# Attention forward and backward with the rows of three heads ordered 32, 32, 32, 8, 8, 8: V and dO rows of heads 0 to 23 copied from the projection pass instead of transposed on PE

## The chip, the cores and the metric

The kernel runs on one core of a Trainium2 chip. The metric is the device time of one execution in microseconds (us), as the median of several executions. Stage times and waits come from the trace of one profiled execution of each kernel.

The engines are called PE (matrix products and transposes), PEld (its weight loads), VectorE (DVE in the profile), ScalarE (ACT), GpSimd (POOL) and SyncE (SP, which only issues transfers). Each works through its own list in order, and they wait for each other by semaphores.

## The reference

A block with segment-wise attention that carries a memory of 8 rows from segment to segment, then a gated linear unit; the kernel computes the output and the gradients of eleven inputs.

```python
S, D, H, E = 2048, 512, 32, 128;  M, T = 8, 32;  L = M + T = 40   # 64 segments
for s in range(64):                                  # attention A
    h = concat([mem, x[s*T:(s+1)*T]])                # 40 rows
    q, k, v = (einsum('btd,dhe->bhte', h, W) for W in (Wq, Wk, Wv))
    p = softmax(where(mask, q @ k.T * E**-0.5, -1e9))
    o = einsum('bhte,hed->btd', p @ v, Wo)
    mem = o[:M]                                      # the next segment needs it
    out.append(o[M:])
x = x + ga * A(layernorm(x) * (1 + ca) + sa)         # ca, sa, ga, ... from silu(c) @ w_mod
x = x + gb * B(layernorm(x) * (1 + cb) + sb)         # B: (sigmoid(h@w_gate) * (h@w_up)) @ w_down
outputs = (x, *vjp(grad_out))
```

Segments depend on each other through `mem` in the forward pass and through its gradient in the backward pass, so both passes are 64 steps one behind the other. What one step's chain takes, the kernel takes 64 times.

## The kernel before

Three heads with 40 rows each make one group of 120 rows; 32 heads (and one pad) make 11 groups. In the forward pass V is projected with rows on partitions (`RA["v"]`), turned by PE into columns per head (`VT`, which the backward pass needs too), and eight of the eleven groups are turned back by PE, this time in group order, into `Vst`, the stationary side of P.V:

```python
                if norms:
                    norms.pop()()                 # GpSimd: Pst of segment s-1 times 1/denominator
                proj("v", 0, "act")
                proj("v", 1, "dve")
                ...
                if 1 <= s4 <= 3:
                    p1(s // nseg_t + P1_AHEAD, s4)   # layer norm of the next tile; s4 = s % 4
                proj("k", 0, "act")
                ...
                self.pop_later()
                st_exp(0)
                vst(0)                            # 4 PE transposes, copied out by VectorE
                st_exp(1)
                vst(1)                            # 4 more
                vst(2)                            # the last three groups
                den(0)
                pv(0)
```

Two pieces of work that come up again are the normalisation on GpSimd and step 2 of the layer norm on VectorE:

```python
                def norm(s=s, Pst=Pst, rden=rden):
                    nc.gpsimd.tensor_tensor(Pst[0:120, :, :], Pst[0:120, :, :], rden..., op=ALU.mult)
                    nc.sync.dma_start(self.PS[s], Pst[:])
            def scale():
                nc.vector.tensor_scalar(xh[:], st["x0"][:], mean, rstd, op0=ALU.subtract, op1=ALU.mult)
                nc.vector.tensor_tensor(xh[:], xh[:], ca1_bc[:], op=ALU.mult)
```

The backward pass does the same with dO (`RAd`, `dOT`, `dOst`). ScalarE copies the turned columns to `dOT`, VectorE multiplies them with O, PE sums these products with a matrix of minus ones on top of dP, and VectorE makes dS:

```python
                to_heads("act", tp[:], 4, 4, 0, 32, 0)   # two ScalarE copies a half: heads 0-23, last heads
                prod(0)          # VectorE: OT *= dOT, groups 0-3
                dp(0)            # PE: dO.V
                dost(0)          # PE: 4 transposes of dO, copied out by ScalarE
                prod(1)
                prod(2)
                ds(0)            # PE: -sum(dO*O); VectorE: dS
```

The softmax here doesn't subtract the row's maximum and nothing guards it: scores larger than these inputs give would overflow.

Of the kernel before, what the change touches and what calls it, by code (L numbers as in the profile page):

```python
# [40 lines left out]
class K:  # L41
# [209 lines left out]
    def pin(self, i0):  # L251

        last = {}
        for ins in self.traced()[i0:]:
            e = ins.engine
            if e in last:
                self.tc.add_manual_dep(ins, last[e].name, mybir.DependencyInfo(
                    mybir.DependencyClass.NoSync, mybir.DependencyReason.DATA), reason="program order")
            last[e] = ins

# [133 lines left out]
    def phase2(self):  # L394
# [13 lines left out]
        with ExitStack() as ctx:  # L408
# [4 lines left out]
            nc.vector.tensor_copy(maskT[0:120, :], self.maskT[:, :])  # L413
# [29 lines left out]
            RB = {x: ptiles("RB" + x, 1, w=9 * 128)[0] for x in "vkq"}  # L443
# [18 lines left out]
            with tc.tile_pool(name="p0", bufs=1) as p0:  # L462
                p1(0, 0)
# [55 lines left out]
            def to_heads(eng, xt, src, i0, n, r0, w, o):  # L519

                s4 = src.rearrange("p i (j r) -> p i j r", r=32)
                d = xt[:, 120 * i0:120 * (i0 + n)].rearrange("p (i j r) -> p i j r", j=3, r=L)
                self.evac(eng, d[:, :, :, r0:r0 + w], s4[:, :, 0:3, o:o + w])
                for a0, n0, dst in ((0, 3, 0), (3, 3, L), (6, 2, 2 * L)):
                    lo, hi = max(a0, i0), min(a0 + n0, i0 + n)
                    if lo < hi:
                        d = xt[:, 960:1320].rearrange("p (i r) -> p i r", r=120)[:, lo - a0:hi - a0]
                        self.evac(eng, d[:, :, dst + r0:dst + r0 + w], s4[:, lo - i0:hi - i0, 3, o:o + w])

            def rows_out(rows, dram, s0, ns):  # L530

                if ns == 1:
                    nc.sync.dma_start(dram[s0, 0:120, 0:8, :].rearrange("(j r) g e -> j r (g e)", r=L)[:, 0:32],
                                      rows[0:96, 0:1024])
                    nc.sync.dma_start(dram[s0, 0:120, 8:11, :].rearrange("(hl r) g e -> r hl (g e)", r=L)[0:32],
                                      rows[96:128, :].rearrange("r (hl x) -> r hl x", hl=3))
                    return
                for j in range(3):
                    nc.sync.dma_start(dram[s0:s0 + 4, L * j + 32:L * j + L, 0:8, :].rearrange("s q g e -> s q (g e)"),
                                      rows[32 * j:32 * j + 32, 0:1024])  # L540
                for hl in range(3):
                    nc.sync.dma_start(dram[s0:s0 + 4, L * hl + 32:L * hl + L, 8:11, :].rearrange("s q g e -> s q (g e)"),
# [5 lines left out]
            def b_pieces(t):  # L548

                bt = btails[t] = {}  # L550

                def proj_b(x, hf):
                    hb = hxs[t][1]
                    pass_half(x, hf, lambda c: hb[:, c, :, :].rearrange("p s q -> p (s q)"), RB[x], ("act", "dve")[hf])
                    if hf == 1 and x != "v":
                        rows_out(RB[x], DR[x], t * nseg_t, nseg_t)

                def turn_b(x):
                    bt[x] = btp.tile([128, 8, 128], BF16, name="b_cols" + x)
                    tps = [turn_half(RB[x], hf) for hf in range(2)]  # L560
# [37 lines left out]

            tails_in("vk", 0)
            i0 = len(self.traced())  # L600
            for s in range(NS):
# [10 lines left out]
                def proj(x, hf, eng):  # L612
                    pass_half(x, hf, lambda c: hT[:, c, :], RA[x], eng)
                    if hf == 1 and x != "v":
# [57 lines left out]
                def outproj(h0, h1):  # L672
                    if at_ps[0] is None:
                        at_ps[0] = psp.tile([128, 512], F32, name="at_ps", tag="p")
                    for h in range(h0, h1):
                        off = (h // 3) * GW + (h % 3) * L
                        self.col_mm(at_ps[0], OT[:, off:off + 32], Wo[:, h, :], n_at[0], H)
                        n_at[0] += 1

                if norms:  # L680
                    norms.pop()()
                proj("v", 0, "act")
                proj("v", 1, "dve")
                if s == NS - 1:
                    nc.sync.dma_start(self.w_up, io["B_w_up"].rearrange("(c p) f -> p c f", p=128))
                    self.mod_bc(None, 2, "", t=self.bcs[2])
                    self.mod_bc(None, 3, "", t=self.bcs[3])
# [4 lines left out]
                if s == NS - 1:  # L692
                    nc.sync.dma_start(self.w_down, io["B_w_down"].rearrange("(fc p) d -> p fc d", p=128))
                    self.mod_bc(None, 4, "", t=self.bcs[4])
# [13 lines left out]
                if s == NS - 1:  # L708
                    self.mod_bc(None, 5, "", t=self.bcs[5])
                    nc.sync.dma_start(self.w_gate, io["B_w_gate"].rearrange("(c p) f -> p c f", p=128))  # L710
                self.pop_later()
                st_exp(0)
                vst(0)
                st_exp(1)
                vst(1)
# [5 lines left out]
                nc.sync.dma_start(Pst[:], ET[:, :], transpose=True)  # L721
                if mod_r:
# [19 lines left out]
                if s + 1 < NS:  # L742
                    tails_in("kvq", s + 1)
# [12 lines left out]
                if s == NS - 1:  # L756
                    self.glu_first = self.glu_load(0, nc.scalar)
# [9 lines left out]
            self.pin(i0)  # L767

    def glu_tiles(self):
# [3 lines left out]
        self.w_gate = self.flat(Wv, 0, n).rearrange("p (c f) -> p c f", c=DC)  # L773
        self.w_up = self.flat(Wv, n, n).rearrange("p (c f) -> p c f", c=DC)
        self.w_down = self.flat(Wk, 0, n).rearrange("p (c d) -> p c d", c=FC)
        self.bcs = {2: self.flat(Wv, 2 * n, 2 * D, F32), 3: self.flat(Wv, 2 * n + 2 * D, 2 * D, F32),
                    4: self.flat(Wk, n, 2 * D, F32), 5: self.flat(Wq, 2 * n, 2 * D, F32)}
        self.w_gateT = self.flat(Wq, 0, n).rearrange("p (c d) -> p c d", c=FC)
        self.w_upT = self.flat(Wq, n, n).rearrange("p (c d) -> p c d", c=FC)
        self.ring_x0 = [self.flat(Wq, 2 * n + 2 * D + i * D, D) for i in range(2)]  # L780
        self.ring_a = [self.flat(Wk, n + 2 * D + i * D, D) for i in range(6)]
        self.ring_dout = [self.flat(Wk, n + 8 * D + i * D, D) for i in range(7)]
# [10 lines left out]
    def phase3(self):  # L793
# [9 lines left out]
        with ExitStack() as ctx:  # L803
            wtp = ctx.enter_context(tc.tile_pool(name="p3wt", bufs=1, reuse_waits="tile"))
            psM = ctx.enter_context(tc.tile_pool(name="p3psM", bufs=4, space=PSUM, reuse_waits="tile"))
# [1050 lines left out]
```

## Time and profile before

| | us |
|---|---|
| time beside the prediction, median of 3 | 3344.8 |
| all 4 runs of it beside the changed kernel, median | 3350.5 (3339.9 to 3357.9) |
| profiled execution | 3355.7 |
| forward pass, first to last output projection | 1042.0 |
| last row fold to first gate product | 39.3 |
| GLU, first gate product to last accumulation | 362.9 |
| GLU weight gradients, to first dO pass | 199.2 |
| backward pass, first to last dO pass | 1031.8 |
| last dO pass to last gradient product of Wo | 196.4 |
| the rest of the weight gradients | 420.1 |

Each stage is the time between the starts of two named PE instructions in the trace. The prediction shows the busy times and PE's waits. First, two GpSimd groups of the page (busy us and mean ns of one, then its idle time ahead of them and who ended it), then all multiplies of `xh` by `ca_bc` on VectorE (count, shortest, median and longest in ns, first and last start).

```profile
L65 POOL COPY vT<-b_colsv 128x24 bf16<-128x24 bf16 (+2 forms) x256 | 49.7, 238 | 581.3 <-DMA VT<-vT 572.2
L760 POOL TENSOR_TENSOR Pst<-Pst,rden 120x1408 bf16<-120x1408 bf16 x64 | 162.2, 2534 | 57.1 <-DMA Pst<-ET 26.7
```

```profile
L365 DVE TENSOR_TENSOR xh<-xh,ca_bc x16: 691/693/694, 14.3 to 938.4; 128x512 f32<-128x512 f32 x16
```

GpSimd spends 572 us waiting for the store of `VT` to land, so all that stands behind it, the normalisation of 2.53 us included, comes late in a segment. The VectorE multiply takes 0.69 us each of its 16 times. Last, VectorE in one backward segment, whose first dO product started at 2195.26 (start, length, what, idle before):

```profile
2197.69 0.42 DVE L63 CAST RAd<-pass_ps 128x256 bf16<-128x256 f32 x1 [0.65 <-ACT RAd L61]
2198.03 0.22 DVE L295 COPY dh_rb<-dh_tp 128x128 bf16<-128x128 bf16 x1
2198.17 0.40 DVE L1335 TENSOR_TENSOR OT_l<-dOT,OT_l 128x480 bf16<-128x480 bf16 x1
2199.48 0.67 DVE L1335 TENSOR_TENSOR OT_l<-dOT,OT_l 128x480 bf16<-128x480 bf16 x2 [0.92 <-ACT dOT L61]
2200.22 0.69 DVE L1360 SCALAR_TENSOR_TENSOR dS<-dp_ps,Pst_l 128x512 bf16<-128x512 f32 x1
```

The first product starts 2.91 us into the segment, ahead of the wait for ScalarE's second half, and the first dS at 4.96.

### The profile page before, as it was taken

Reading aid. Unit: us, or ns where it says so; the run is one execution under the profiler, and the core shown is the slowest. Engines: PE = TensorE matmul, PEld = TensorE weight load, DVE = VectorE, ACT = ScalarE, POOL = GpSimd, SP = SyncE. Lnnn points to the kernel's source line nnn. Section 1 sums busy time; section 2 is a strip of 40 time slices with the busy share of each in tenths; the row PEclk is TensorE's granted clock in tenths of the full one; section 3 lists DMA queues with packets and bytes.
Section 4 is the critical chain, followed back from the end, with each engine's and each line's share of the span. In section 5 each row is a group of like instructions: output and inputs, shape, how many; then the busy total and the mean of one; then the engine's idle time right before and its main releaser. Section 6 shows DMA issues by size and latency. Waiting matters only on the chain. (4 is left out here: it accounts for less than half of the span.)

```text
span 3355.7 us, 97380 instructions
## 1 busy us (share of the span) xinstructions
PE 3060.2 (91%) x39662; PEld 1791.3 (53%) x39662; DVE 1644.5 (49%) x4158; ACT 1225.7 (37%) x2842; POOL 1061.3 (32%) x2262
## 2 busy tenths in 40 slices
PE   6999999999998699988989999999999988999999
PEld 3566666565555344444555555555555543445454
DVE  5666666666665567653244445555554442322221
ACT  3444554444444333322134444444444430100111
POOL 2344443333333355540122222222222221332321
PEclk8999999999999899999999999999999998999999
DMA  8788877878777788887779999999999999877685
GB/s 280 156 164 162 161 163 162 158 159 158 155 154 153 201 201 199 203 242 246 228 186 240 245 242 242 246 241 249 243 243 242 239 240 230 242 198 208 181 228 161
DMA packets 862317, 692.22 MB, mean 206 GB/s; under 512 B 562198, under 2 KB 737574, under 8 KB 861740
## 3 DMA queue, kind: packets, MB, share of 16 engines
q1 hardware_dynamic: 768624, 503.21, 67.5%
q0 software_dynamic: 39488, 135.58, 12.0%
q10 hardware_dynamic: 53756, 47.19, 5.3%
q8 instruction: 312, 5.11, 0.7%
q14 instruction: 137, 1.12, 0.1%
HBM read 292.29 MB, written 275.02 MB: 169 GB/s over the span
## 5 line engine op out<-in xcount | busy, mean ns | idle before, releaser
L1663 PE MATMUL gps<-rows,hrows 128*128 128x512 bf16 (+2 forms) x2160 | 417.0, 355 | 0.0
L1663 PEld LDWEIGHTS <-hrows 128*128 128x128 bf16 x2160 | 211.2, 98 | 204.2
L222 PEld LDWEIGHTS <-hT 128*32 128x32 bf16 x6144 | 179.5, 97 | 173.4 <-issue 39.6
L65 POOL COPY vT<-b_colsv 128x24 bf16<-128x24 bf16 (+2 forms) x256 | 49.7, 238 | 581.3 <-DMA VT<-vT 572.2
L63 DVE CAST ot<-gps 128x512 bf16<-128x512 f32 (+3 forms) x76 | 48.2, 635 | 340.8 <-PE gps L1663 231.4
L272 DVE TENSOR_TENSOR dh_lo<-dh_ps,dh_hi 128x256 bf16<-128x256 f32 x128 | 48.4, 420 | 316.3 <-ACT dh_hi L268 316.3
L760 POOL TENSOR_TENSOR Pst<-Pst,rden 120x1408 bf16<-120x1408 bf16 x64 | 162.2, 2534 | 57.1 <-DMA Pst<-ET 26.7
L61 ACT ACTIVATE ot<-gps 128x512 bf16<-128x512 f32 (+3 forms) x75 | 41.2, 550 | 360.0 <-PE gps L1663 260.8
L1667 POOL DMA_DIRECT2D out_dram<-ot x108 | 81.2, 752 | 286.1 <-DVE ot L63 143.2
L222 PE MATMUL pass_ps<-Wv,hT 128*32 128x512 bf16 x2048 | 126.0, 388 | 29.7 <-ACT hT L752 29.7
L1381 POOL DMA_DIRECT2D DVR<-rows_x x64 | 34.5, 540 | 371.9 <-DMA rows_x<-dVT 371.9
L222 PE MATMUL pass_ps<-WoT,dyT 128*32 128x512 bf16 x2048 | 124.1, 384 | 27.9 <-ACT dyT L1466 27.9
L61 ACT ACTIVATE dQT<-g_ps 128x512 bf16<-128x512 f32 (+1 forms) x192 | 94.0, 562 | 151.5 <-issue 149.2
L1673 PE MATMUL gps5o<-WoT,rows 128*128 128x512 bf16 x600 | 134.2, 385 | 4.4 <-DMA rows<-OSR 4.4
L662 DVE TENSOR_TENSOR Ost<-or_ps,rden 120x512 bf16<-120x512 f32 (+1 forms) x192 | 124.3, 647 | 21.7 <-PE dc_ps L639 1.7
L1360 DVE SCALAR_TENSOR_TENSOR dS<-dp_ps,Pst_l 128x512 bf16<-128x512 f32 (+1 forms) x192 | 118.3, 644 | 24.0 <-PE dp_ps L1358 19.5
L222 PE MATMUL pass_ps<-Wk,hT 128*32 128x512 bf16 x2048 | 123.8, 382 | 0.0
L222 PE MATMUL pass_ps<-Wq,hT 128*32 128x512 bf16 x2048 | 122.4, 379 | 0.0
L211 PE MATMUL at_ps<-Wo,OT 128*32 128x512 bf16 x2048 | 122.3, 380 | 0.0
L211 PE MATMUL dh_ps<-WkT,dKT 128*32 128x512 bf16 x2048 | 122.3, 380 | 0.0
L211 PE MATMUL dh_ps<-WvT,dVT 128*32 128x512 bf16 x2048 | 122.3, 380 | 0.0
L211 PE MATMUL dh_ps<-WqT,dQT 128*32 128x512 bf16 x2048 | 121.6, 379 | 0.0
(383 smaller groups left out, 7115.9 us busy)
## 6 DMA issues: line engine op xcount, KB each, us to landing
OSR<-Ost SPq DMA_DIRECT2D x64, 352.0 KB
OT<-OT SPq DMA_DIRECT2D x64, 352.0 KB
PS<-Pst SPq DMA_DIRECT2D x64, 352.0 KB
OT_l<-OT SPq DMA_DIRECT2D x64, 352.0 KB
Pst_l<-PS SPq DMA_DIRECT2D x64, 352.0 KB
DVR<-rows_x POOLq DMA_DIRECT2D x64, 352.0 KB, 4.5
DKR<-rows_x POOLq DMA_DIRECT2D x64, 352.0 KB, 4.9
DQR<-rows_x POOLq DMA_DIRECT2D x64, 352.0 KB, 3.7
```

The costliest lines, as they stand in the source:

```text
L61: return nc.scalar.activation(out, in_, AF.Copy)
L63: return nc.vector.tensor_copy(out, in_)
L65: return nc.gpsimd.tensor_copy(out, in_)
L211: self.nc.tensor.matmul(ps[32 * j:32 * j + 32, :], lhsT=lhsT, rhs=w, start=(n < 4), stop=(n >= total - 4), tile_position=(0, 32 * j))
L222: self.nc.tensor.matmul(ps[32 * j:32 * j + 32, :], lhsT=lhs(c), rhs=rhs, start=(c == 0), stop=(c == DC - 1), tile_position=(0, 32 * j))
L272: nc.vector.tensor_tensor(lo[:], ps[:, 256 * h:256 * h + 256], parts[h][:], op=ALU.subtract)
L662: nc.vector.tensor_tensor(part3(Ost, pi)[0:120, 0:n, :], or_ps[0:120, 0:n, :], rden[:, pi * PG:pi * PG + n].unsqueeze(2).to_broadcast([120 ...
L760: nc.gpsimd.tensor_tensor(Pst[0:120, :, :], Pst[0:120, :, :], rden[:, :].unsqueeze(2).to_broadcast([120, G, 128]), op=ALU.mult)
L1360: nc.vector.scalar_tensor_tensor(out=part3(dS, pi), in0=ps[:, 0:n, :], scalar=cfg.scale, in1=part3(Pst, pi), op0=ALU.mult, op1=ALU.mult)
L1663: nc.tensor.matmul(ps[:, 0:ng * E], lhsT=hrows[:, tp_, c * 128:(c + 1) * 128], rhs=rows[:, tp_, 0:ng * E], start=(tp_ == 0), stop=(tp_ == ...
L1667: nc.gpsimd.dma_start(outw[c * 128:(c + 1) * 128, h0:h0 + 3 * (ng - 1) + 1:3, :], ot[:, 0:ng * E].rearrange("p (h e) -> p h e", e=E))
L1673: nc.tensor.matmul(ps[:], lhsT=rows[:, tp_, gg * E:(gg + 1) * E], rhs=dyrows[:, tp_, :], start=(tp_ == 0), stop=(tp_ == NTP - 1))
```

## The change

Its intent: with the 120 rows of a group ordered as 32 memory-and-token rows of three heads and then their 8 last rows, the first 96 rows are in `Vst` exactly as the projection pass puts them on partitions. GpSimd copies them over, the 24 tail rows come by three small transfers, and 8 PE transposes with their copies go, in the forward pass and again for dO in the backward pass. The row stores of Q and K become contiguous. At the seams between stages several loads and waits move. The core of it:

```diff
-                if norms:
-                    norms.pop()()
                 proj("v", 0, "act")
+                nc.gpsimd.tensor_copy(Vst[0:96, 0:512], RA["v"][0:96, 0:512])
                 proj("v", 1, "dve")
+                nc.gpsimd.tensor_copy(Vst[0:96, 512:1024], RA["v"][0:96, 512:1024])
+                if norms:
+                    norms.pop()()
 ...
                 st_exp(0)
-                vst(0)
                 st_exp(1)
-                vst(1)
                 vst(2)
 ...
+                    v_tails(s + 1)          # three transfers of 8 rows x 1024
 ...  rows_out: 3 x 32 x 1024 becomes 96 x 1024
-  nc.sync.dma_start(dram[s0, 0:120, 0:8, :].rearrange("(j r) g e -> j r (g e)", r=L)[:, 0:32], rows[0:96, 0:1024])
+  nc.sync.dma_start(dram[s0, 0:96, 0:8, :].rearrange("r g e -> r (g e)"), rows[0:96, 0:1024])
 ...  backward pass
-                d = dOT[:, 960 + L * i0:960 + L * (i0 + n)]...
-                self.evac(eng, d[:, :, r0:r0 + w], s4[:, :, 3, o:o + w])
+                for g in range(3):                       # last heads: two pieces a half
+                    lo, hi = max(3 * g, i0), min(3 * g + 3, i0 + n, 8)
+                    if lo < hi:
+                        self.evac("pool" if eng == "pool" else "dve", ...)
 ...
+                    nc.gpsimd.tensor_copy(dOst[0:96, 512 * hf:512 * hf + 512], RAd[0:96, 512 * hf:512 * hf + 512])
 ...
                 dp(0)
-                dost(0)
                 prod(1)
 ...
                 dp(1)
-                dost(1)
```

Cut here: the last segment issues its loads on other queues (GLU weights on GpSimd's, rows on SyncE's); the GLU's memory plan and a fifth PSUM buffer; the staging of the attention weights; the first product of the Wo gradients split in three parts, with its rows loaded in pieces; and a pin of the order of SyncE's and ScalarE's loads in the weight gradients.

## The prediction

> **What bounds the kernel now.** I read the page first, then busy time by stage, then PE's waits stage by stage, then PE beside ScalarE and VectorE inside one segment. From the page:
>
> ```profile
> PE 3060.2 (91%) x39662; PEld 1791.3 (53%) x39662; DVE 1644.5 (49%) x4158; ACT 1225.7 (37%) x2842; POOL 1061.3 (32%) x2262
> PEclk8999999999999899999999999999999998999999
> ```
>
> PE is the bound on average, and nothing else is near; but its clock dips three times, at the seams between stages. Busy time by stage (window and its length, PE, PEld, DVE, ACT, POOL in us, then clock, DMA share, GB/s):
>
> ```profile
> 60.00:1105.00 1045.00, 957.47 (x16895) 625.65 (x16896) 633.40 (x1997) 512.06 (x1282) 403.46 (x1076) 1.00 0.78 160
> 1105.00:1700.00 595.00, 518.93 (x3023) 263.70 (x3026) 307.30 (x546) 166.01 (x288) 231.76 (x266) 0.95 0.77 212
> 1700.00:2776.00 1076.00, 985.10 (x16512) 607.43 (x16504) 531.96 (x1251) 468.54 (x1151) 266.00 (x671) 0.99 1.02 241
> 2776.00:3355.00 579.00, 567.21 (x2833) 278.24 (x2833) 142.72 (x279) 62.90 (x90) 150.41 (x204) 0.99 0.77 208
> ```
>
> These are attention forward (64 segments, 16.3 us each), the GLU, attention backward (64 segments, 16.8 us each) and the weight gradients. PE idles 88, 76, 91 and 12 us in them. The waits of PE, taken window by window (total us, times, longest):
>
> ```profile
> PE tps L648 <- DVE Ost L662: 37.7, 109, 0.6
> PE pass_ps L222 <- ACT hT L752: 28.6, 60, 0.8
> ...
> PE ao_b_ft L281 <- ACT ao_b_hi L268: 14.8, 1, 14.8
> ...
> PE acc_ps L1006 <- POOL pr_ga L1000: 9.6, 12, 1.5
> PE mm L909 <- DVE du L934: 5.3, 11, 1.1
> ...
> PE gps L1031 <- DMA Wk<-HHROWS: 7.2, 1, 7.2
> PE pass_ps L222 <- POOL dyb L1244: 4.7, 1, 4.7
> ...
> PE dh_tps L211 <- POOL dh_tail L1732: 10.6, 1, 10.6
> PE gps5o L1673 <- DMA WoT<-zrow: 4.7, 1, 4.7
> ```
>
> Inside a segment the waits are short and recur (a dependent chain through VectorE or ScalarE); at the seams there are four single waits of 5 to 15 us. Now one forward segment, first PE, then ScalarE, then VectorE (start, length, what):
>
> ```profile
> 612.25 0.43 PE L648 MATMUL tps<-ident,vT 128*128 128x128 bf16 x4
> ...
> 613.01 0.55 PE L648 MATMUL tps<-ident,vT 128*128 128x128 bf16 x7
> 613.40 0.24 PE L639 MATMUL dc_ps<-ones,ET 128*128 128x1 bf16 x4
> ...
> 612.50 0.60 ACT L629 ACTIVATE ET<-st_ps 128x480 bf16<-128x480 f32 x1
> ...
> 613.43 0.42 DVE L63 COPY Vst<-tps 128x512 bf16<-128x512 bf16 x1 [0.24 <-PE tps L648]
> ```
>
> The reader sees that 7 transposes take 0.39 us from their start to the next block's, so 0.056 us each; that the exponential of the first score tile ends at 613.10, only 0.30 us before the denominators start; and that VectorE is still copying a V tile when they do.
>
> **What the Trainium skill says.** "TensorE: Matmul & The Clock Gate", Back-to-back issue gap and Part 1: a 128-column matmul costs N/2.4 + 2.5 ns when warm, and about 3.4 us of idling halves the clock. The trace agrees: 56 ns per transpose, and the dips of the clock follow the waits of 14.8 and 10.6 us. "GPSIMD Engine Reference", 4.1 Engine selection: one-input work is roughly at line rate there. The trace agrees: a Pool copy of 264 columns takes 0.41 us and one of 96 columns 0.27 us, so I estimate 0.65 us for 512. "SBUF — State Buffer", Who interferes with whom: a VectorE instruction with two SBUF inputs contends with a Pool instruction that reads SBUF; no line of this profile shows it yet. "DMA: Bandwidth & Descriptors", on why a DMA increments its semaphore by 16: a DMA runs on the largest k up to 16 that divides the slowest dimension of both sides. The row stores of K and Q go from 3x32x1024 to 96x1024, so from 3 engines to 16; the profile doesn't name engines, so it can't confirm this.
>
> **The change part by part.** The compiled programs differ by 1,023 matmuls: 64 segments x 8 transposes x 2 directions, less one added for the mask. The ceiling is 1,024 x 0.056 = 57 us.
>
> *Forward segments.* Removed: 8 transposes (0.45 us PE) and two VectorE copies (0.83 us). Added: two Pool copies of 96x512 (1.3 us) and three small Pool DMAs (0.54 us each, as its other DMA issues take): 2.9 us of Pool, busy 6.3 of 16.3 us now. Pool has room, and PV comes over 5 us after the V pass, so I put nothing of it on the path. But PE doesn't get all of 0.45: the denominators can't start before the exponential is out, at about 613.2, so 0.2 us earlier. VectorE, free of its copies, starts the reciprocal and the first product about 0.3 us earlier, and the three products of 0.69, 0.69 and 0.56 us with their reciprocals set the end. I take 0.32 us x 63 = 20 us, and 4 more for segments where VectorE also serves the next tile's layer norm: 24 us.
>
> *Forward to GLU.* ScalarE sits behind DMA issues that wait for buffers, so PE waits 14.8 us. Those loads go to the sync queue a segment earlier, the weights to Pool's queue. From the end of the forward part (1105.3) to the first GLU matmul (1140.8) are 35.5 us. I estimate 15 to 16: about 10 of transposes that stay, 5 for layer norm and its DMA transpose. The three weights, 5.5 MB at the stage's 214 GB/s, take 26 us and then set the start unless issued 10 us before the seam. Gain 20 us.
>
> *GLU.* The order of the program puts the accumulation that waited for Pool's pr_ga behind the next gate products, and there is a fifth PSUM buffer. A steady iteration takes 20.5 us, of which PE works 18.9. I take 1 us x 13 = 13 us.
>
> *GLU weight gradients, start of backward.* The 7.2 us wait for HHROWS and the 4.7 us wait for dyb go, with some 3 us at half clock behind them, less 1 for loads that now show: 14 us.
>
> *Backward segments.* Removed: 8 transposes (0.45 us) and two ScalarE copies (1.1 us). Added: Pool as before, and four small VectorE copies for the last heads (some 0.16 us each). VectorE lies on the path: products, then dS of 0.69, 0.65 and 0.5 us, then the last transposes of dS. Following one segment by hand I get the three dS done 0.1 us earlier to 0.1 later and the gradient matmuls 0.25 us earlier; a quarter of the segments, where ScalarE also evacuates the tails, should gain 0.5. 64 x 0.31 = 20 us.
>
> *Backward to weight gradients.* Waits of 10.6 (tail copies behind a DMA issue on Pool), 4.7 (zero rows) and 4.4 us (rows<-OSR), each followed by half clock: 40 matmuls there take 402 ns each where 216 is usual. Of the 25 us I expect 19; loading the next rows takes the rest.
>
> Set-up adds about 1 us. Sum: 24 + 20 + 13 + 14 + 20 + 19 - 1 = 109 us. 3344.8 - 109.8 gives **3235 us**, 3.3% less.
>
> **The rivals.** (1) Pool becomes the bound. Its forward order is tails of K, V, Q, then V copies, then the norm; the V tails wait 542 us in total (9 us per segment) for the store of VT. If that landing comes no earlier, Q's tails and then the V copies arrive just at the scores, which already waited on Pool three times (1.5 us in all). For: slack there is some 0.6 us. Against: the stores spread over more engines. It would give back 0.3 to 0.6 us per segment: 3255 to 3270. (2) The chains through VectorE and ScalarE hide all of the transposes: both segment gains vanish, only the seams count, 3280. Against: VectorE is itself relieved in the forward part. (3) DMA: share 1.02 in the backward part. Against: PE waited for no DMA there. If it limits, 20 us go: 3255. (4) The seams don't shrink, as weights or rows land late: 3265 to 3275. Upward, full transposes and full seams would make 3195.
>
> **Range and chances.** No single rival brings it over 3278, the 2% line; two together do. 8 in 10: 3195 to 3285. Faster by over 2%: 0.86; within 2%: 0.13; slower: 0.01.
>
> **What would show it.** Right: forward and backward stages shorter by about 24 and 20 us; PE's wait on VectorE's Ost unchanged or larger; no PE wait over 5 us at the first, second and last seam; GLU iterations near 19.4 us. Wrong: PE waits on Pool for Vst, dOst or qT; on a DMA in the backward part; a forward stage as long as before; a first gate product later than 20 us after the last forward product.

## The result, and the profile after

| | before | after |
|---|---|---|
| median, 4 runs each | 3350.5 | 3385.6 |
| range | 3339.9 to 3357.9 | 3380.7 to 3390.6 |
| ratio | | 1.0107, 95% interval 1.0072 to 1.0143 |

Ratios, here and below, are the mean time of one kernel's runs over the mean of the other's runs of the same rounds, so not quite the ratio of the medians. The change made the kernel 1.1% slower where 3.3% faster was predicted. By stage, from the two profiled executions:

| stage | before | after | predicted | measured |
|---|---|---|---|---|
| forward pass | 1042.0 | 1049.8 | -24 | +7.7 |
| to first gate product | 39.3 | 40.0 | -20 | +0.6 |
| GLU | 362.9 | 355.4 | -13 | -7.5 |
| GLU weight gradients | 199.2 | 197.0 | -14 | -2.2 |
| backward pass | 1031.8 | 1046.4 | -20 | +14.6 |
| to the end of the Wo gradients | 196.4 | 211.8 | -19 | +15.5 |

Forward code that is the same in three kernels below took 1048.2 to 1050.0 us, so differences of 2 us in that stage are scatter; for the kernel before, two such profiles gave 1042.0 and 1048.7. So the loss in the forward pass is somewhere between nothing and 8 us. Backward code that is the same took 1042.3 to 1046.5 us against a single 1031.8 before, so that loss, 10 to 15 us, is clear. The GLU scatters more: its code before the change took 362.9 and 356.5 us in two profiles, the changed code 342 to 358 in all the kernels below, and the GLU weight gradients took 193 to 204 in all kernels. The -7.5 and -2.2 lie within that.

The page of the changed kernel and its stages (windows cut at the ends of the stages, columns as in the prediction):

```profile
PE 3033.4 (90%) x38639; PEld 1729.5 (51%) x38639; DVE 1670.1 (49%) x4292; ACT 1136.6 (34%) x2586; POOL 1442.3 (43%) x3038
```

```profile
60.00:1109.00 1049.00, 942.58 (x16367) 590.79 (x16355) 628.50 (x1869) 508.79 (x1282) 586.25 (x1391) 0.99 0.58 162
1109.00:1702.00 593.00, 517.82 (x3099) 265.92 (x3099) 310.45 (x552) 167.82 (x291) 231.78 (x270) 0.95 0.79 212
1702.00:2773.00 1071.00, 971.78 (x15972) 578.45 (x15965) 559.71 (x1507) 382.31 (x893) 456.37 (x1116) 1.00 1.05 243
2773.00:3384.00 611.00, 570.01 (x2833) 278.54 (x2832) 143.29 (x279) 61.98 (x90) 154.12 (x209) 0.97 0.82 202
```

PE is busy 27 us less (the prediction put the transposes that went at 57), and yet the span is longer: PE waits more. In the forward pass the DMA share fell from 0.78 to 0.58 at the same GB/s. PE's waits over the whole kernel:

```profile
PE tps L680 <- DVE Ost L694: 35.6, 97, 0.7
PE turn_ps L231 <- DVE RA0q L63: 31.7, 14, 2.3
PE dp_ps L1406 <- DVE OT_l L1383: 27.4, 65, 0.9
...
PE mm L945 <- DVE du L966: 18.6, 13, 2.8
PE tp L862 <- DVE Wq L63: 17.8, 3, 16.9
...
PE acc_ps L1610 <- DMA dhb<-DHB: 15.3, 3, 9.0
PE gps5o L1737 <- DMA rows<-OSR: 14.1, 1, 14.1
...
PE wtp L1208 <- DMA won<-in_A_Wo_dram: 6.8, 2, 4.4
...
PE wtp L1195 <- DMA wn<-in_A_Wk_dram: 6.0, 3, 3.4
...
PE wtp L1195 <- DMA wn<-in_A_Wv_dram: 3.8, 2, 3.3
```

The old seam waits (14.8, 10.6, 7.2, 4.7 us) are gone or, in the case of the 7.2, down to 2.7. In their place stand waits that were not there: 14 times 2.3 us for VectorE's copy of Q, a wait in nearly every backward segment for the products dO*O (0.4 us on average, 0.9 at most), and single waits for weights, rows and transfers at each seam.

**The forward pass.** By segment number modulo 4, over the later segments, a segment took 16.79, 16.28, 16.38, 16.49 us before and 16.21, 15.95, 17.85, 15.70 after. Three classes gain 0.33 to 0.79 us (0.32 predicted); one, the class s mod 4 = 2, loses 1.5 us. In such a segment, first GpSimd, then VectorE:

```profile
485.16 0.61 POOL L713 COPY Vst<-RA0v 96x512 bf16<-96x512 bf16 x1 [1.99 <-ACT RA0v L61]
486.13 0.86 POOL L715 COPY Vst<-RA0v 96x512 bf16<-96x512 bf16 x1 [0.36 <-DVE RA0v L63]
486.96 2.53 POOL L790 TENSOR_TENSOR Pst<-Pst,rden 120x1408 bf16<-120x1408 bf16 x1
```

```profile
485.98 0.54 DVE L374 TENSOR_SCALAR xh<-x,mv,rstd 128x512 f32<-128x512 bf16 x1
486.56 3.49 DVE L375 TENSOR_TENSOR xh<-xh,ca_bc 128x512 f32<-128x512 f32 x1
489.97 0.68 DVE L63 CAST RA0k<-pass_ps 128x512 bf16<-128x512 f32 x1
490.57 0.67 DVE L63 CAST RA0q<-pass_ps 128x512 bf16<-128x512 f32 x1
```

The multiply that took 0.69 us before takes 3.49 us: it ends 0.56 us after GpSimd's normalisation, which itself takes its usual 2.53, although it had started 0.41 us before the normalisation, while GpSimd's second V copy still ran (0.86 us, against 0.61 for the first). So it is in 14 of the 16 tiles. Both read two SBUF tensors. VectorE then copies K and Q out 2.8 us late, and PE waits for them. The same view as before, over all 16 tiles:

```profile
L375 DVE TENSOR_TENSOR xh<-xh,ca_bc x16: 692/3490/3492, 14.7 to 951.8; 128x512 f32<-128x512 f32 x16
```

**The backward pass.** VectorE in a segment that started at 2202.83:

```profile
2205.75 0.29 DVE L63 COPY dOT<-turn_ps 128x96 bf16<-128x96 bf16 x2
2205.96 0.21 DVE L305 COPY dh_rb<-dh_tp 128x128 bf16<-128x128 bf16 x1
2207.12 0.29 DVE L63 COPY dOT<-turn_ps 128x64 bf16<-128x64 bf16 x2 [0.94 <-ACT dOT L61]
2207.32 0.97 DVE L1383 TENSOR_TENSOR OT_l<-dOT,OT_l 128x480 bf16<-128x480 bf16 x3
2208.21 1.95 DVE L1408 SCALAR_TENSOR_TENSOR dS<-dp_ps,Pst_l 128x512 bf16<-128x512 f32 x3
```

The four small copies of the last heads stand ahead of the products. The second pair waits for ScalarE's copy of the second half, so even the first product, which needs only the first half, starts 4.49 us into the segment instead of 2.91, and dS at 5.38 instead of 4.96.

**The seam to the GLU.** GpSimd of the changed kernel:

```profile
1129.13 2.53 POOL L790 TENSOR_TENSOR Pst<-Pst,rden 120x1408 bf16<-120x1408 bf16 x1 [22.61 <-DMA Pst<-ET]
...
1133.34 2.28 POOL L897 TENSOR_TENSOR db<-Wv 128x512 bf16<-128x512 bf16 x2
...
1140.18 1.16 POOL L897 TENSOR_TENSOR db<-Wk,Wv 128x512 bf16<-128x512 bf16 x1 [3.51 <-DMA hdT<-db]
...
1142.23 0.58 POOL L910 TENSOR_TENSOR rstd<-ve,mhalf 128x1 f32<-128x1 f32 x1
```

The last segment's normalisation waits 22.6 us for its transposed tile, a third `db` product waits for a transfer, and only then comes the small `rstd`, for which VectorE has waited 17.5 us. The copy of a weight transpose stands behind that on VectorE, and PE waits 16.9 us for it.

**The seam to the weight gradients.** The first Wo product starts 11.8 us after the last backward product instead of 28.4, as intended, but the second set of rows has not landed (14.1 us), then `dhb` is late (15.3 us), and at the end of the Wo gradients the kernel is 15.5 us behind.

### The profile page after: what moved, and what is told of

It is laid out like the page before. It is cut to its first block, busy times and chain, and to the rows that moved or that the text cites. A ratio compares the mean times of both kernels' runs of the same rounds, so it can differ in the third digit from the quotient of the medians. Undisturbed runs are those within 1.5% of the kernel's fastest.

```text
span 3384.2 us, 95734 instructions
## 1 busy us (share of the span) xinstructions
PE 3033.4 (90%) x38639; PEld 1729.5 (51%) x38639; DVE 1670.1 (49%) x4292; ACT 1136.6 (34%) x2586; POOL 1442.3 (43%) x3038
## 5 line engine op out<-in xcount | busy, mean ns | idle before, releaser
L222 PEld LDWEIGHTS <-hT 128*32 128x32 bf16 x6144 | 158.9, 97 | 185.0 <-ACT hT L784 30.5
L790 POOL TENSOR_TENSOR Pst<-Pst,rden 120x1408 bf16<-120x1408 bf16 x64 | 162.0, 2531 | 22.6 <-DMA Pst<-ET 22.6
L1737 PE MATMUL gps5o<-WoT,rows 128*128 128x512 bf16 x600 | 137.6, 393 | 17.2 <-DMA rows<-OSR 14.1
L1453 POOL COPY dOst<-RAd 96x512 bf16<-96x512 bf16 x128 | 78.2, 617 | 92.3 <-DVE RAd L63 91.9
```

The costliest lines, as they stand in the source:

```text
L222: self.nc.tensor.matmul(ps[32 * j:32 * j + 32, :], lhsT=lhs(c), rhs=rhs, start=(c == 0), stop=(c == DC - 1), tile_position=(0, 32 * j))
L1453: nc.gpsimd.tensor_copy(dOst[0:96, 512 * hf:512 * hf + 512], RAd[0:96, 512 * hf:512 * hf + 512])
L1737: nc.tensor.matmul(pss[gg][:], lhsT=rows[:, tp_, gg * E:(gg + 1) * E], rhs=dyrows[:, tp_, :], start=(tp_ == order[0]), stop=(tp_ == order[ ...
```

## The experiments

Fourteen kernels ran, each correct, each timed in three rounds against the kernel before. Diffs are abbreviated. "Forward" and "backward" are the stages of the table above.

| kernel | median | ratio to before, 95% interval | forward | backward |
|---|---|---|---|---|
| changed kernel | 3385.6 | 1.0107 [1.0072, 1.0143] | 1049.8 | 1046.4 |
| norm_late | 3340.7 | 0.9952 [0.9932, 0.9971] | 1008.6 | 1046.5 |
| norm_early | 3331.8 | 0.9930 [0.9909, 0.9951] | 1010.7 | 1044.8 |
| prod_first | 3373.7 | 1.0044 [1.0009, 1.0080] | 1050.0 | 1043.0 |
| ds0_first | 3416.0 | 1.0174 [1.0152, 1.0196] | 1048.2 | 1079.5 |
| dyb_vector | 3339.6 | 0.9934 [0.9911, 0.9957] | 1008.0 | 1049.9 |
| small_scalar | 3325.4 | 0.9884 [0.9859, 0.9910] | 1003.8 | 1035.6 |
| dyb_start | 3311.2 | 0.9853 [0.9825, 0.9882] | 1006.9 | 1017.2 |
| before_small | 3381.1 | 1.0052 [1.0009, 1.0095] | 1048.7 | 1051.8 |
| turns_back | 3360.6 | 0.9990 [0.9965, 1.0016] | 1023.8 | 1053.9 |
| seams | 3324.8 | 0.9892 [0.9868, 0.9915] | 1007.3 | 1042.3 |
| glu_order | 3315.1 | 0.9862 [0.9832, 0.9892] | 1007.9 | 1044.8 |
| together | 3286.9 | 0.9787 [0.9752, 0.9822] | 1003.3 | 1018.1 |
| together_turns | 3319.4 | 0.9896 [0.9870, 0.9921] | 1022.1 | 1032.8 |
| together_late | 3337.1 | 0.9941 [0.9906, 0.9976] | 1051.7 | 1028.8 |

### The forward pass: where the normalisation stands

`norm_late` moves one line of the changed kernel, `norm_early` moves it the other way:

```diff
 # norm_late
                 nc.gpsimd.tensor_copy(Vst[0:96, 512:1024], RA["v"][0:96, 512:1024])
-                if norms:
-                    norms.pop()()
 ...
                 self.pop_later()
+                if norms:
+                    norms.pop()()
                 st_exp(0)
 # norm_early
+                if norms:
+                    norms.pop()()
                 proj("v", 0, "act")
                 nc.gpsimd.tensor_copy(Vst[0:96, 0:512], RA["v"][0:96, 0:512])
```

> The changed kernel with one line moved: GpSimd's normalisation of Pst (2.53 us on two SBUF tiles) is issued behind the row store in the middle of a segment instead of right behind the V copies. V copies, tail transfers and everything else stay. Theory A (collision): in the changed kernel the forward segments with s mod 4 = 2 take 17.85 us against 15.70 to 16.21 of the others, because VectorE's multiply of xh by ca_bc (0.69 us alone) takes 3.49 us while that normalisation runs. Then the multiply should be back at about 0.7 us, those segments at 15.7 to 16.1 us, the forward pass (first to last output projection) at about 1015 us instead of 1049.8, and the whole kernel about 30 us shorter, at 3350 to 3360. Rival B: the 2 us are the price of the V copies and tail transfers on GpSimd, which stay: then no change of the forward pass (within 4 us) and a total within 0.3% of the changed kernel.

> The same one-line move in the other direction: the normalisation is issued ahead of the two V copies, at the start of the segment, some 2 us before VectorE's multiply begins. Theory A: again no collision, segments with s mod 4 = 2 at 15.7 to 16.1 us, forward pass about 1015 us, total 3350 to 3360; the V copies end about 1 us later, which has slack of some 8 us until the first P.V product. Rival B (GpSimd's own load is the cost): V copies come later still, so no gain or a loss. If only the late placement gains and this one not, something else than the overlap of these two instructions decides.

Both did what the collision theory asked. The segments with s mod 4 = 2 fell from 17.85 to 15.78 and 15.76 us, the others stayed within 0.22 us, and the forward pass got 41 and 39 us shorter. The multiply in `norm_early`:

```profile
L375 DVE TENSOR_TENSOR xh<-xh,ca_bc x16: 692/978/979, 14.8 to 911.2; 128x512 f32<-128x512 f32 x16
```

Its median is 0.98 us and no longer 3.49; the 0.29 us over 0.69 go with the V copy that still runs beside it. With the V copies and tail transfers still on GpSimd, the rival is refuted: the cost was the overlap of the multiply with the normalisation behind the V copies. No run has the normalisation there without the copies, so whether it needs a copy to hold the multiply until it starts is not shown. The kernel before had the normalisation at the head of the segment in program order, and its wait for `VT` put it behind the multiply in time; the change moved it behind the V copies, where nothing holds it any longer. The kernels got 45 and 54 us shorter (medians), more than the 30 expected and more than the pass; in `norm_early` the GLU stage was 10 us shorter too (345.3 against 355.4), which nothing here explains.

### The backward pass: the small copies on VectorE

`prod_first` keeps the first pair of small copies ahead and moves the second pair behind two products. `ds0_first` moves all four, and the third product, behind the first dS:

```diff
 # prod_first
                 prod(0)
                 dp(0)
                 prod(1)
+                last_heads(second half)
                 prod(2)
                 ds(0)
 # ds0_first
                 prod(1)
-                prod(2)
                 ds(0)
+                last_heads(first half); last_heads(second half)
+                prod(2)
```

> The changed kernel with the second pair of VectorE's small dOT copies (last heads, 64 and 32 columns) moved behind the first two products dO*O; the first pair stays ahead. Theory A (order on VectorE): the first product starts about 1 us earlier in each of 64 backward segments; the wait of PE for OT_l (26.5 us in total) falls below 10; a segment gets 0.1 to 0.3 us shorter, the backward pass (1046.4 us) shrinks by 6 to 20 us. Rival B: ScalarE's dOT evacuation of the second half sets dS either way, since all three products still end in series behind it: then under 4 us.

> As the run before, and further: all four small copies and the third product stand behind the first dS instruction on VectorE, so that dS of the first four head groups waits for two products and no small copy. Theory A: first dS 0.8 us earlier than in the changed kernel, backward segments 0.3 to 0.5 us shorter each (16.55 to about 16.1), backward pass 20 to 32 us shorter, below that of the kernel before (1031.8) by 5 to 18. Rival B (the dS chain is set by PE or ScalarE): within 5 us of the changed kernel's 1046.4.

`prod_first`: the wait for OT_l fell from 25.5 to 0.6 us inside the pass, and three of four classes of segments got 0.38 to 0.48 us shorter (16.17, 16.72, 16.59 to 15.70, 16.34, 16.11). But the class that computes the tail rows of the next four segments rose from 16.72 to 17.78: PE waited 19.0 us for `dyb`, a GpSimd copy that stood behind a wait of 9.9 us for a transfer. The pass got only 3.4 us shorter.

`ds0_first` was a miss, 33 us slower. The reason is in PE's waits of it:

```profile
PE dp_ps L1403 <- DVE dOT L63: 42.4, 60, 0.8
```

On PE the products dO.V of the last groups stand ahead of the second and third set of sums, so everything there waited for the copies I had put behind dS. What I took for slack on VectorE was on PE's path.

The next three take `norm_early` as their base, so that the forward pass is settled. `dyb_vector` has the order of `prod_first` and makes `dyb` on VectorE inside the segment that needs it; `small_scalar` gives the small copies to ScalarE instead; `dyb_start` is `small_scalar` with `dyb` as VectorE's first instruction of the segment.

```diff
 # small_scalar, dyb_start
-                        self.evac("pool" if eng == "pool" else "dve", ...)     # last heads of dOT
+                        self.evac(eng, ...)
 # dyb_start; dyb_vector and small_scalar have get_db further down, in front of proj_b
+                if s4 == 2 and s > 3:
+                    get_db(s // 4 - 1)                # on VectorE
```

> norm_early, with the order of prod_first in the backward pass, and the copy dyb (128x128, tail rows of the next four segments' gradient) on VectorE at the start of the segment that needs it, instead of on GpSimd at the end of the segment before. In prod_first three of four segment classes got 0.38 to 0.48 us shorter (16.17, 16.72, 16.59 to 15.70, 16.34, 16.11) but one went from 16.72 to 17.78 because PE waited 19.0 us for dyb, which GpSimd made late behind a wait of 9.9 us for the transfer rows_x. Theory A (order on VectorE cost the backward pass its gain, and dyb ate what the new order gave): wait for dyb gone, all classes at or below 16.35 us, backward pass 1015 to 1025 us, total about 25 us under norm_early (3305 to 3312). Rival B: transfers bound the backward pass (DMA is at 90% or more there), so the slack moves to another wait on a load or a store: backward pass stays above 1038 us.

> As dyb_vector, but instead of the new order on VectorE the four small copies of the last heads are made by ScalarE, right behind each half's dOT copy. VectorE then has nothing ahead of the first product. Theory A: PE's wait for OT_l gone, but ScalarE's second dOT copy comes about 0.4 us later (two small copies at an estimated 0.2 us each, from the 128x32 ACTIVATE that takes 0.20 us), so dp waits for ScalarE instead: 0.1 to 0.3 us a segment better than norm_early, less than dyb_vector. If better than dyb_vector, VectorE's total load and not its order is what counts.

> small_scalar with the copy dyb made by VectorE as the first instruction of the backward segment that needs it. In small_scalar and dyb_vector it stood behind other work of that segment and PE still waited 17.1 and 21.4 us for it, so the class of segments with it stayed at 17.49 and 18.26 us while the others fell to 15.55, 16.32 and 16.03. Theory A (place in VectorE's order): the wait for dyb falls below 3 us, that class to about 16.3 us, the backward pass to about 1015 us (small_scalar: 1035.6), 16 us below the kernel before. Rival B (the load of daq lands late because transfers fill the pass, at a DMA share of 1.0): VectorE now waits for daq at the head of the segment, the class stays above 17 us and the backward pass within 6 us of 1035.

`dyb_vector` seemed to speak for the rival that transfers bound the pass: 1049.9 us, and PE still waited for `dyb`. But the three other classes were at 15.67, 16.32 and 16.16, and in the trace `dyb` stood behind the copies and the waits of its own segment. `dyb_start` settled it. PE's waits in the backward pass of `dyb_start` (1700 to 2650):

```profile
PE dp_ps L1400 <- ACT dOT L61: 25.5, 56, 0.5
PE pass_ps L222 <- ACT dyT L1520: 21.4, 59, 0.9
PE dp_ps L1408 <- DVE OT_l L1385: 4.3, 10, 1.0
```

No wait for `dyb`, that class at 16.19 us, the pass at 1017.2: 29 us under the changed kernel and 15 under the kernel before, while transfers took no smaller a share (1.11 in this window, 1.05 in the changed kernel's backward stage). The pass was not bound by them. `small_scalar` also showed that ScalarE, relieved of two of its three dOst copies, takes the small copies better than VectorE does; I had expected less of it than of `dyb_vector`.

`before_small` is the reverse check: one part of the change alone, put into the kernel before.

```diff
-                self.evac(eng, d[:, :, r0:r0 + w], s4[:, :, 3, o:o + w])
+                self.evac("pool" if eng == "pool" else "dve", d[:, :, r0:r0 + w], s4[:, :, 3, o:o + w])
```

> The kernel before with one part of the change alone: in the backward pass the copy of the last heads' columns of dOT (one per half) is made by VectorE instead of ScalarE. No transpose is removed, no row order changed. By the theory that these copies ahead of the products dO*O cost the backward pass its gain, the segments get 0.2 to 0.35 us longer, the backward pass 12 to 22 us (1031.8 to 1044 to 1054), the kernel 0.4 to 0.7% slower. By the rival (row order, tail transfers or GpSimd copies cost it) nothing changes within 3 us.

The backward pass rose from 1031.8 to 1051.8 us and every class by 0.28 to 0.31 us. No transpose and no row order had changed, so the place of these copies ahead of the products costs as much by itself as was to be gained.

### What the transposes are worth

`turns_back` puts the transposes back into `norm_early` and takes out the GpSimd copies and tail transfers; `together_turns` does so with `together` (below) as base.

```diff
-                nc.gpsimd.tensor_copy(Vst[0:96, ...], RA["v"][0:96, ...])      # both, and v_tails, dO_tails
                 st_exp(0)
+                vst(0)
                 st_exp(1)
+                vst(1)
 ...
                 dp(0)
+                dost(0)
 ...
                 dp(1)
+                dost(1)
```

> norm_early with the PE transposes of V and dO put back (8 each per segment) and without the GpSimd copies and the small tail transfers; row order, row stores and seams stay those of the changed kernel. It measures what the transposes themselves are worth. By the prediction's steps a forward segment should be 0.32 us longer (16.04 to 16.36, forward pass +20 us). In the backward pass, by the prediction +0.31 us a segment; by the theory that the wait for the dO*O products fills their place, under 0.1 us a segment (within 6 us of 1045). Rival for the forward pass: the gain came from the shorter row stores and not from the transposes, then under +0.1 us there too.

> together with the PE transposes of V and dO put back and the GpSimd copies and tail transfers taken out. It measures the worth of the transposes where the new waits are gone. By the prediction's steps: forward segments +0.32 us (turns_back measured +0.21), backward segments +0.31 us, so +33 to +40 us in all (3287 to 3320 to 3327). By the rival (the dS chain on VectorE and ScalarE fills the freed time in the backward pass anyway): backward +0.05 to +0.15 us a segment and a total of +18 to +23 us.

With the transposes a forward segment took 0.21 us more in `turns_back` (16.25 to 16.04), and 0.30 us more in `together_turns` (the pass rose by 18.8 us in 63 steps). A backward segment took 0.15 us more while VectorE's order still held the products, and 0.23 us more in `together_turns` (14.7 us in 63 steps). So the exchange (transposes and their PSUM copies for GpSimd copies and tail transfers) is worth 33.5 us net of the 44 predicted for both passes, when nothing stands in its way. The forward pass of `turns_back` is 18 us shorter than that of the kernel before with the same transposes: that part comes from something else in the change, row order, row stores or the freed queue; I did not take these apart.

### The seams

`seams` is `norm_early` with the last normalisation issued two GLU iterations later (its tile moved to free weight memory) and without the pin of load order in the weight gradients. `glu_order` adds an order on GpSimd: each `db` product and the moved normalisation behind the `rstd` of the tile before.

```diff
-            norms.pop()()
+            self.last_norm = norms.pop()          # called in the GLU behind iteration 2
 ...
-                    if i == 2:
-                        self.pin(i0, [SP, Activation])
 # glu_order
                 nc.gpsimd.tensor_tensor(db[:], st["dout"][:], gb_bc[:], op=ALU.mult)
+                if j:
+                    self.behind_rstd(that instruction)
```

> norm_early with two seams changed. Seam forward to GLU: the last segment's Pst and rden live in a part of Wq that is free by then, and its normalisation on GpSimd is issued two GLU iterations later, so rstd of the first GLU tile doesn't stand behind a 22.6 us wait for the Pst transfer. If that queue on GpSimd is what held VectorE (17.5 us wait for rstd in the changed kernel) and with it PE (17.3 us for the Wq copies), the first gate product comes 10 to 17 us sooner after the last row fold (36.7 us to 20 to 27). Rival: weights arriving at the same time set it, then under 4 us. Seam backward to weight gradients: the pin of load order is taken out, so w_mod is not fetched ahead of the rows. If load order costs the 15 us there, from the end of the backward pass to the last o product falls by 5 to 15 us (198 us); if the 45 MB that have to be moved in that stretch bound it, within 4 us.

> seams, in which the first gate product came no sooner (39.1 us after the last row fold): there GpSimd still had the third db product, which waits for the transpose transfer of the first one, and the moved normalisation ahead of the first rstd, so VectorE waited 19.9 us for rstd. Here each db product from the second on, and the moved normalisation, are ordered behind the rstd of the tile before. Theory A (GpSimd's order holds VectorE and PE): first gate product 22 to 30 us after the last row fold. Rival (weights and rows land late): within 4 us of 37. The rest of the kernel as in seams (3324.8), so the total is 10 to 15 us less, or the same.

At the first seam `seams` gained nothing: 39.1 us to the first gate product (`norm_early` 36.7), for the normalisation was issued just as early as before, and the third `db` still stood ahead of `rstd`. GpSimd of `seams`:

```profile
1083.30 2.53 POOL L796 TENSOR_TENSOR Wq<-Wq 120x1408 bf16<-120x1408 bf16 x1 [9.27 <-DMA Wq<-ET]
...
1096.49 1.15 POOL L903 TENSOR_TENSOR db<-Wk,Wv 128x512 bf16<-128x512 bf16 x1 [6.44 <-DMA hdT<-db]
...
1098.55 0.59 POOL L916 TENSOR_TENSOR rstd<-ve,mhalf 128x1 f32<-128x1 f32 x1
```

`glu_order` mended that and came to 34.8 us, 4.3 less, not the 22 to 30 of the theory. PE's wait for VectorE fell to 6.2 us, and in its place VectorE waits 5.0 us for rows from memory and GpSimd 6.4 us for `grad_out`. GpSimd's order is a part of what holds this seam; late rows are another. The rest is in the order of SyncE: the last wait of PE ahead of the first gate product is for a transfer that turns the first tile of `h`. VectorE had that tile ready at 1083.55, but SyncE issued the transfer 14.6 us later, behind 30 loads. PE's wait, VectorE's instruction and SyncE's issue in `glu_order`:

```profile
PE mm L954 <- DMA hdT<-h: 9.9, 1, 9.9
1082.87 0.68 DVE L931 TENSOR_TENSOR h<-h2a,Wv 128x512 bf16<-128x512 f32 x1
1098.15 1.20 SPq L938 DMA_TRANSPOSE hdT<-h  x1
```

In the changed kernel the same transfer was issued as soon as `h` was ready, so there GpSimd's order was the limit. No run moves the transfer ahead of the loads, so what that would gain is not shown.

At the second seam the theory of load order held: from the end of the backward pass to the end of the Wo gradients 211.0 us in `norm_early`, 201.8 in `seams` and 202.5 in `glu_order`. What remains is what the kernel before took (196.4, and 201.8 in `before_small`), so an earlier start gained nothing there.

### Together, and the collision put back

`together` is `dyb_start` with `glu_order`. `together_late` is `together` with the normalisation behind the V copies again, as the change has it.

> All of norm_early, dyb_start and glu_order in one kernel. If the collision in the forward pass, the order on VectorE in the backward pass and GpSimd's order at the GLU start are separate causes, their gains add: the changed kernel 3385 minus 40 (forward), minus 30 (backward), minus 12 (start of the GLU), minus 9 (load order of the weight gradients) is about 3290 to 3300, a ratio of 0.975 to 0.985 to the kernel before. If transfers bound the whole, the gains do not add and it stays above 3310.

> together with only GpSimd's normalisation put back behind the V copies, as the change has it. If the collision is the whole loss of the forward pass: segments with s mod 4 = 2 from 15.57 to 17.8 us, others unchanged, forward pass from 1003 to about 1040 us, total 3287 to 3320 to 3327. If the collision needs something else that together mended, less than 10 us.

`together` takes 3286.9 us: 2.1% less than the kernel before and faster than both. The interval, 0.9752 to 0.9822, is clear of 1 but not of the 2% line. Ratio to the changed kernel, worked out from the two ratios: 0.9787 / 1.0107 = 0.968. The gains of the parts added up. Of what was predicted for the change itself, about 52 us are still missing, most of them at the seams: `together` has the forward pass 38.7 us under the kernel before and the backward pass 13.7, but the first seam only 4.0, and the GLU weight gradients and the Wo gradients are 4.7 and 3.6 longer. Its forward and backward stages:

```profile
60.00:1062.00 1002.00, 926.45 (x16346) 577.88 (x16335) 593.27 (x1866) 506.84 (x1280) 580.88 (x1391) 1.00 0.59 170
...
1644.00:2687.00 1043.00, 966.51 (x15980) 576.07 (x15980) 551.91 (x1265) 410.78 (x1150) 461.11 (x1102) 0.99 1.09 250
```

The backward stage has the DMA share at 1.09 and more GB/s than the changed kernel (250 to 243), and is shorter. `together_late` brought the whole loss back: segments with s mod 4 = 2 from 15.57 to 18.03 us, the forward pass from 1003.3 to 1051.7, the kernel to 3337. That is 48 us in the pass and 50 in all, more than the 33 to 40 I had expected.

## Why the prediction was wrong

**Forward segments (predicted -24, measured +7.7).** The term for the transposes was about right: 0.32 us a segment predicted, 0.30 measured in `together_turns` and 0.21 in `turns_back`. Some 18 us that the forward pass gained besides (`turns_back` against the kernel before) had no term, so -24 would have been passed by luck without the loss. The step that failed is the one on GpSimd: "Pool has room, and PV comes over 5 us after the V pass, so I put nothing of it on the path", and on contention, "no line of this profile shows it yet". The Trainium skill, "SBUF — State Buffer", section "Who interferes with whom", says that the shared port pair is an exclusive lock, held for a whole instruction, and that a VectorE instruction with two SBUF inputs contends with a GpSimd instruction that reads SBUF. The trace agrees that the two contend and that the loser is held to the end: 3.49 us instead of 0.69, ending 0.56 us behind the 2.53 us normalisation. By start times the multiply came 0.41 us ahead of the normalisation and was still the one held; but a V copy was running then, and the normalisation followed it directly. And the profile before did show such a line, in the GLU (shortest, median and longest in ns):

```profile
L959 DVE TENSOR_TENSOR pr_gb<-Wk,b_bf x16: 411/1376/5408, 1168.8 to 1487.4; 128x512 bf16<-128x512 bf16 x16
```

This product of two SBUF tensors takes 0.41 us alone and 1.38 in the 12 of 16 iterations where GpSimd's product `pr_ga` runs beside it. I had read the rule, overlooked this line, and did not ask which instructions the diff would bring together in time. The change removed GpSimd's 572 us wait for `VT` and moved the normalisation to just where VectorE multiplies two SBUF tensors; that cost 39 us (`norm_early`) to 48 (`together_late`).

**Backward segments (predicted -20, measured +14.6).** The transposes were worth 0.23 us and not 0.31. The step that failed is "Following one segment by hand I get the three dS done 0.1 us earlier to 0.1 later". I had counted the four small copies by their length (0.16 us each; measured 0.16 to 0.21) and not by their place: ahead of the first product on an engine that works in order, and the second pair waits for ScalarE. In the segments shown the first product came 1.58 us later and the first dS 0.42 later; by the median of all 64 segments 1.11 and 0.59, and the end of the last dS 0.37; `before_small` shows 20 us for such copies alone.

**Forward to GLU (predicted -20, measured +0.6).** The wait behind ScalarE went, and a wait behind GpSimd took its place. The step "about 10 of transposes that stay, 5 for layer norm and its DMA transpose" left out that `rstd` is made on GpSimd, behind a normalisation that waits for a transfer, and that the weights' transposes and the layer norm share VectorE. Mending the order gave 4 us; of what keeps it at 35 us, the trace of `glu_order` shows the last 9.9 us as the wait for the layer norm's turned tile, issued late on SyncE. So "5 for layer norm and its DMA transpose" was also too small. My fourth rival named this outcome, with late weights as the reason; the trace has the last weight landed at 1128.0, and VectorE still stood until 1142.9.

**GLU (predicted -13, measured -7.5).** The mechanism was right: PE's wait for pr_ga fell from 12.2 to 1.5 us. The size was off by the wait for `du`, which rose from 11.8 to 18.6 us (16 to 23 in all kernels with the change, 12.7 in `before_small`). The stage times themselves scatter by more than the 5.5 us missed.

**GLU weight gradients (predicted -14, measured -2.2).** Both waits shrank or went (7.2 to 2.7, 4.7 to none in this stage), but the staging loads of the attention weights, which had had that time to land, now show: 16.6 us of waits for `won` and `wn` (6.8 + 6.0 + 3.8) against 7.6 before. "Less 1 for loads that now show" was the mis-sized term. No experiment was made on it, and the -2.2 lies within the scatter, so this is read from waits alone.

**Backward to weight gradients (predicted -19, measured +15.5).** The start did come 16.7 us sooner. "Of the 25 us I expect 19; loading the next rows takes the rest" failed: the next rows take it all, and the pinned load order another 9.

**The rivals and the range.** The first (GpSimd as the bound) named the engine but the wrong way: PE waits little on GpSimd (0.8 us for `dOst`, none for `Vst`), VectorE was locked out by it. The second (chains hide the transposes) and the third (DMA limits the backward pass) are refuted by `together_turns` and `dyb_start`. "No single rival brings it over 3278" counted only what I had listed, and not even that, as the second rival stood at 3280; the two largest losses, some 39 and 20 us, were not among them. Of the signs I had named for being wrong, two came: a forward pass as long as before, and a first gate product about 44 us after the last forward product instead of 20. Smaller slips changed little: the terms add up to 109, not 109.8; only two of the three dips of the clock are at seams, the first is the start of the program; and the "402 ns each" of 40 matmuls holds a wait of 4.4 us, while most of them were 216 ns apart.

## What to carry to other kernels

When a change relieves a wait on GpSimd, ask where its long two-input instruction will now fall in time, and which VectorE instruction with two SBUF inputs lies there: here a lock cost VectorE 2.8 us, somewhat more than the length of GpSimd's instruction (2.53) and not of its own (0.69), and it counted because PE waited for what stood behind it. To find such pairs in a profile, look for VectorE instructions with two SBUF inputs whose longest time is far above their shortest. A small copy costs its place in an engine's order and what it waits for, not its length; put it behind the work that someone on the path waits for, or on the engine that the change relieved, and check that no other engine then waits for it in its own order. A wait removed at a seam is a gain only if the next load has landed by then.

## What the Trainium skill lacked or had wrong

- "SBUF — State Buffer", "Who interferes with whom", was right that such a pair contends. What it leaves open is who goes next when GpSimd's instructions follow each other: in 14 of 16 tiles the multiply started 0.41 us ahead of the normalisation, while another GpSimd copy ran, and yet ended 0.56 us behind it (3.49 us against 0.69). What it costs is not there either: 14 such holds of some 2.8 us cost the forward pass 39 us, 1.2% of the kernel, and in the kernel before, with the same two instructions in it, none.
- No page has the cost of place of a small copy: four VectorE copies of 96, 64 and 32 columns out of PSUM took only 164 to 208 ns each, and ahead of the products they made a backward segment 0.3 us longer (`before_small`).
- "DMA: Bandwidth & Descriptors" gives the rule for how many engines serve a transfer; what it means for a profile is not there: with the row stores at 96x1024 in place of 3x32x1024, the DMA share of the forward pass fell from 0.78 to 0.58 at 160 and 162 GB/s. `turns_back`, which has the row order and the row stores but not the GpSimd copies and tail transfers, also has 0.55 at 163 GB/s, so it goes with the rows. The number of engines itself no trace shows.
